# Window attention, max-MoE and gated MoE in one kernel: 256x256 weight tiles, a 16-bit sign word, low parts on VectorE, and another order

## The chip, the core and the metric

The kernel runs on one core of one Trainium2 chip. The core has a matrix engine (TensorE, PE in the profile; its weight loads are shown apart as PEld), a vector engine (VectorE, DVE), a scalar engine (ScalarE, ACT), GpSimd (POOL) and SyncE (SP), which issues nearly all DMAs here. They run side by side and wait for each other by semaphores. The metric is the device time of one execution in microseconds (us).

## What is computed

Three stages follow each other. All inputs are float64 and reach the kernel as pairs of 32-bit words; the output is float32.

```python
# attention, batch 4, 8 heads, 512 local + 32 global rows, head size 64
s_g = scale * q_g @ concat(k_g, k_l).T;  out_g = softmax(s_g) @ concat(v_g, v_l)
s_l = concat(scale * q_l @ k_g.T, where(|i-j| <= 32, scale * q_l @ k_l.T, -1e9))
out_l = softmax(s_l) @ concat(v_g, v_l)
x = concat(out_g, out_l)                     # 2176 tokens x 512
# max-MoE, d_ff 768
h = maximum(maximum(x @ w1, x @ w2), x @ w3);  x = h @ w_out
# gated MoE, d_ff 1536
out = (sigmoid(x @ w_gate) * (x @ w_val)) @ w_out2
```

## The kernel before

**Work units.** The attention is cut into 32 units: batch, half of the local rows, and pair of heads (four units make one chunk `c`; there are eight chunks). The max-MoE takes a chunk at a time, as soon as its four units are done. So the first two stages run interleaved, and the gated MoE follows them.

**A unit.** For chunks 0 and 1, TensorE transposes rows of q and k (`tq`, `tk`, L532), VectorE and ScalarE copy them out (`qw` L553, `kw` L557), TensorE makes the scores (`sp`, L619), VectorE adds the mask and takes the minimum of the negated scores (`sm`, `st`, L625: four main instructions, "reductions" below, each with an accumulator read), ScalarE takes the exponentials (L661, four) and scales their sum (L665), VectorE takes the reciprocal (L667) and multiplies (L675). TensorE transposes the result (`tp`, L683, two halves of four matmuls), ScalarE copies one half out (`pw`, L686) and VectorE the other (`pw`, L688). TensorE multiplies by the values (`ot`, L770), and ScalarE writes the unit's part of x (L790 for chunk 0, whose max-MoE runs on whole float32 values; L796 and L798 split it into a high and a low part for the others). The global rows have their own small products (`sg`, `tpg`, `ogw`).

**The weights of the max-MoE.** `w1`, `w2`, `w3` are 512 x 768 and `w_out` is 768 x 512, in float64. `conv_a(i)` brings one tile in by a DMA on SP (L302, L305) and makes it float32 in `to_f32`: ScalarE shifts the low word (L285) and scales the high word (L289), VectorE puts the sign of the high word into the low word (L291) and shifts the two together (L294). Chunk 0 uses that value. For the other chunks ScalarE rounds it to a high part (L312) and the helper `sub` subtracts the high part on GpSimd (L271), which leaves the low part; three matmuls (`mm3`, L321 to L323: high-high, high-low, low-high) then take the place of one. A tile of w1 to w3 holds all 512 rows (four blocks of 128) of 128 columns, 512 values in each of the 128 partitions. There are 24 tiles, 18 of w1 to w3 and 6 of w_out. In a product of layer 1 (`moe1_l1`, L882 for chunk 0) the four blocks of one tile meet the four parts of x; its maximum with the other two products is taken on VectorE (`h` L896, `hw` L893). Layer 2 (`moe1_l2`) follows, L918 for chunk 0. The gated MoE also uses `to_f32`, with 1024 values in a partition.

**The order.** Every step is an event, and a step issues a few instructions on their engines. The table `ORDER` at the top lists the numbers of all events; each engine runs its instructions in that order, and waits only where data or buffers are not ready. `SLOT` places the buffers.

Of the kernel before, what the change touches and what calls it, by code (L numbers as in the profile page):

```python
# [12 lines left out]
U32 = mybir.dt.uint32  # L13
AF = mybir.ActivationFunctionType
ALU = mybir.AluOpType
# [188 lines left out]
def kernel(  # L204
# [76 lines left out]
    def to_f32(raw, low_on_act, out=None):  # L281
# [4 lines left out]
        else:  # L286
            nc.vector.tensor_scalar(out=lo, in0=lo.bitcast(U32), scalar1=2.0 ** -29, scalar2=7.0, op0=ALU.mult, op1=ALU.min)
        yield
        nc.scalar.mul(f32(hi), f32(hi), 2.0 ** -112)  # L289
        yield  # L290
        nc.vector.scalar_tensor_tensor(out=lo, in0=hi, scalar=-2147483648, in1=lo,  # L291
                                       op0=ALU.bitwise_and, op1=ALU.bitwise_or)
        yield
        nc.vector.scalar_tensor_tensor(out=hi if out is None else out, in0=hi, scalar=3, in1=lo,  # L294
# [1182 lines left out]
```

## Time and profile before

| what | value |
|---|---|
| time, median of 3 runs | 809.6 us (809.15 to 814.51) |
| the profiled execution's own time | 812.87 us |
| its span, first to last instruction | 811.0 us |
| mean granted TensorE clock | 0.996 of full speed |
| PE busy | 788.9 us, 6854 matmuls |
| DVE busy | 599.6 us |
| ACT busy | 472.7 us |
| POOL busy | 148.8 us |

The span is the part that the profile resolves; 1.9 us of the execution lie around it. Times of rows are counted from the span's start. A busy PE need not be at its peak, since matmuls are pipelined. In rows of a timeline consecutive instructions of one kind are merged (x8 is eight of them; one float32 matmul of the program shows as two records). "Idle before" names what ended an engine's wait.

### The profile page before, as it was taken

What the parts mean: (1) busy time and instruction counts of PE and PEld (TensorE: products, weight loads), DVE (VectorE), ACT (ScalarE), POOL (GpSimd) and SP (SyncE); (2) the same over time, 40 slices, a digit from 0 to 9 for tenths busy, and PEclk for the clock granted to TensorE, in tenths of its full rate; (3) what the DMA queues carried; (4) which work ended last, traced back from release to release, by engine and by line L of the source; (5) the groups of instructions that cost most, each with busy time, mean ns of one, the idle gap of its engine ahead of it and who ended that gap; (6) DMA issues with size and microseconds to landing.
All of it is one profiled execution on the core that took longest, in us unless ns stands there. A gap on an engine that the chain in (4) does not pass through costs nothing.

```text
span 811.0 us, 18055 instructions
## 1 busy us (share of the span) xinstructions
PE 788.9 (97%) x6854; PEld 751.8 (93%) x6854; DVE 599.6 (74%) x1291; ACT 472.7 (58%) x1131; POOL 148.8 (18%) x149
## 2 busy tenths in 40 slices
PE   5999998999999999999999999999999999999998
PEld 3687798998999999899999999999999999999998
DVE  4799895876767676874876888788675858967773
ACT  6897775756446664563647656665636366444442
POOL 3241565243332413332120000000000000000000
PEclk9899999999999999999999999999999999999999
DMA  8998254545556553453425355956422469555411
GB/s 202 265 248 212 60 101 87 102 93 104 107 101 109 96 113 66 101 117 75 181 90 191 101 158 175 317 175 231 147 101 91 163 207 311 166 162 164 142 34 58
DMA packets 217590, 116.07 MB, mean 143 GB/s; under 512 B 161056, under 2 KB 204576, under 8 KB 217504
## 3 DMA queue, kind: packets, MB, share of 16 engines
q1 hardware_dynamic: 216960, 114.80, 52.2%
q8 instruction: 53, 0.87, 0.5%
q14 instruction: 33, 0.27, 0.1%
q10 hardware_dynamic: 544, 0.13, 0.1%
HBM read 74.91 MB, written 28.57 MB: 128 GB/s over the span
## 4 chain that ended last, share of the span: by engine, by line
PE 73%; SPq 8%; issue 6%; DMA 5%; DVE 3%; POOL 2%; ACT 2%; DVEq 0%; POOLq 0%; ACTq 0%
PE pa L1038 18%; PE pe L1038 9%; PE pa L1225 9%; PE ps L321 7%; PE ps L323 7%; PE ps L322 6%; PE pb L1038 4%; PE pe L1225 4%; PE pb L1225 2%; SPq L514 2%; SPq L513 2%; PE sp L619 2%; DMA vr<-in_v_g_dram 1%; PE ps L918 1%; POOL m L271 1%
## 5 line engine op out<-in xcount | busy, mean ns | idle before, releaser
L1038 PE MATMUL pa<-m,m 128*128 128x384 f32 (+1 forms) x864 | 154.1, 327 | 0.0
L321 PE MATMUL ps<-xt,m 128*128 128x288 f32 (+1 forms) x504 | 147.4, 292 | 3.5 <-DVE h L896 2.2
L323 PE MATMUL ps<-xt,m 128*128 128x288 f32 (+1 forms) x504 | 146.6, 291 | 0.0
L322 PE MATMUL ps<-xt,m 128*128 128x288 f32 (+1 forms) x504 | 145.3, 288 | 1.1 <-DVE xt L798 0.9
L1038 PEld LDWEIGHTS pa<-m,m 128*128 128x128 f32 x864 | 144.3, 188 | 0.2
L321 PEld LDWEIGHTS ps<-xt,m 128*128 128x128 f32 x504 | 94.8, 188 | 7.8 <-issue 2.7
L322 PEld LDWEIGHTS ps<-xt,m 128*128 128x128 f32 x504 | 94.7, 188 | 1.5 <-DVE xt L798 1.1
L323 PEld LDWEIGHTS ps<-xt,m 128*128 128x128 f32 x504 | 94.7, 188 | 0.0
L1044 ACT COPY sn<-pa 128x384 f32<-128x384 f32 (+1 forms) x108 | 49.0, 462 | 73.0 <-PE pa L1038 72.6
L1038 PE MATMUL pe<-m,m 128*128 128x384 f32 (+1 forms) x432 | 80.2, 327 | 0.0
L1038 PEld LDWEIGHTS pe<-m,m 128*128 128x128 f32 x432 | 72.5, 188 | 0.1
L1225 PE MATMUL pa<-m,m 128*128 128x256 f32 x576 | 71.9, 283 | 0.0
L1225 PEld LDWEIGHTS pa<-m,m 128*128 128x128 f32 x576 | 70.4, 192 | 0.1
L661 ACT ACTIVATE sm<-sm,st 128x224 f32<-128x224 f32 x128 | 60.8, 481 | 13.3 <-DVE st L625 13.0
L896 DVE TENSOR_TENSOR h<-ps,h 128x288 f32<-128x288 f32 (+1 forms) x90 | 38.9, 436 | 34.9 <-PE ps L323 23.5
L271 POOL TENSOR_TENSOR h<-h,h 128x288 fp32r<-128x288 f32 (+1 forms) x42 | 39.4, 942 | 103.1 <-ACT h L901 102.6
L707 DVE TENSOR_TENSOR pc<-sm,pc 64x512 f16<-64x512 f32 (+1 forms) x72 | 52.0, 723 | 8.1 <-ACT pc L704 6.9
L625 DVE CUSTOM_DVE_ANT_0 sm<-sp,mask 128x224 f32<-128x224 f32 x128 | 44.9, 381 | 7.9 <-PE sp L619 7.4
L321 PE MATMUL ps<-h,m 128*128 128x288 f32 (+1 forms) x168 | 49.4, 294 | 0.0
L1163 ACT CAST m<-m 128x768 fp32r<-128x768 f32 x44 | 35.8, 835 | 23.0 <-DVE m L1174 7.5
L704 ACT CAST pc<-sm 64x512 f16<-64x512 f32 (+1 forms) x72 | 39.3, 545 | 16.7 <-DVE sm L675 15.1
L323 PE MATMUL ps<-h,m 128*128 128x288 f32 (+1 forms) x168 | 48.9, 291 | 0.0
(193 smaller groups left out, 1628.7 us busy)
## 6 DMA issues: line engine op xcount, KB each, us to landing
m<-in_moe_w_dram SPq DMA_DIRECT2D x18, 512.0 KB, 5.5
gd<-sgt SPq DMA_DIRECT2D x48, 192.0 KB, 2.8
m<-gd SPq DMA_DIRECT2D x6, 1536.0 KB, 7.3
m<-in_moe_w_val_dram SPq DMA_DIRECT2D x6, 1024.0 KB, 5.3
wr<-in_moe_w_out_dram SPq DMA_DIRECT2D x6, 1024.0 KB, 6.0
m<-in_moe_w_gate_dram SPq DMA_DIRECT2D x5, 1024.0 KB, 7.6
vr<-in_v_l_dram SPq DMA_DIRECT2D x48, 96.0 KB, 2.5
x2d<-x2s SPq DMA_DIRECT2D x32, 128.0 KB, 2.0
```

The costliest lines, as they stand in the source:

```text
L271: nc.gpsimd.tensor_tensor(out=out, in0=a, in1=f32(b), op=ALU.subtract)
L321: nc.tensor.matmul(ps, lhsT=wh, rhs=xh, start=first, stop=False)
L322: nc.tensor.matmul(ps, lhsT=wh, rhs=xl, start=False, stop=False)
L323: nc.tensor.matmul(ps, lhsT=wl, rhs=xh, start=False, stop=last)
L625: nc.vector.tensor_tensor_reduce(out=sm[:, hh, j], in0=sp[hh][:, j, 0:224], in1=mask[:, half + j, :], scale=-SC, scalar=3.0e38, op0=ALU.ad ...
L661: nc.scalar.activation(sm4[:, i], sm4[:, i], AF.Exp, bias=st[:, 0, i:i + 1], scale=-1.0, accum_out=st[:, 2, i:i + 1])
L704: nc.scalar.copy(d, s_)
L707: nc.vector.tensor_tensor(out=l_, in0=s_, in1=h_, op=ALU.subtract)
L896: nc.vector.tensor_tensor(out=a, in0=ps[:, 0:n], in1=a, op=ALU.max)
L1038: nc.tensor.matmul(ps, lhsT=w[l][:, a, i], rhs=x[m][:, i], start=(k in (1, 2, 5) and i + l + m == 0), stop=(k in (2, 3, 4) and i == 1 and ...
L1044: nc.scalar.copy(t[:, 0:n], pend[u]["a"][:, 0:n])
L1225: nc.tensor.matmul(ps, lhsT=g[l][:, f], rhs=wo_op(b, f, m), start=(k in (1, 2, 5) and f + l + m == 0), stop=(k in (2, 3, 4) and f == 5 and ...
```

## The change

Four things change.

1. A tile of w1 to w3 becomes 256 rows by 256 columns, still 512 values in a partition. Its DMA reads rows of 2048 bytes where it read 1024. A product of layer 1 now reads two tiles (the two row halves of a column pair), and two products share a pair. The order of tiles in the queue is that of the event table.
2. The sign step works on 16-bit words: a one-source operation copies the top half of the high word, masked to its sign bit, into the top half of the low word. It was a two-source operation on 32-bit words. The same helper serves the gated MoE.
3. The 24 subtractions that make the low parts of the max-MoE weights are issued on VectorE where GpSimd did them. The subtractions of `h` (L271) stay on GpSimd.
4. The whole table `ORDER` is another one (a first line of each stands in the diff).

```diff
-    153, 154, 57, 87, 0, 256, 56, 62, 63, 64, 67, 68, 69, 74, 58, 70, 71, 59, 1854, 161, 162, 95, 96, 75, 76, 77, 78,
+    56, 57, 0, 62, 63, 64, 67, 223, 68, 69, 74, 75, 58, 59, 70, 76, 71, 77, 5, 161, 162, 163, 6, 7, 8, 9, 171, 78, 79,
...
@@ to_f32
-        nc.vector.scalar_tensor_tensor(out=lo, in0=hi, scalar=-2147483648, in1=lo,
-                                       op0=ALU.bitwise_and, op1=ALU.bitwise_or)
+        half = raw.bitcast(U16)
+        nc.vector.tensor_scalar(out=half[:, :, 1], in0=half[:, :, 3], scalar1=0x8000, scalar2=None, op0=ALU.bitwise_and)
...
@@ conv_a
+        fp, kh = divmod(f, 2)
...
-            nc.sync.dma_start(out=raw.rearrange("p (k f) t -> p k (f t)", k=KD),
-                              in_=src[:, f * 2 * P:(f + 1) * 2 * P].rearrange("(k p) f -> p k f", p=P))
+            nc.sync.dma_start(out=raw.rearrange("p (k f) t -> p k (f t)", k=2),
+                              in_=src[kh * 2 * P:(kh + 1) * 2 * P, fp * 4 * P:(fp + 1) * 4 * P].rearrange("(k p) f -> p k f", p=P))
...
-        sub(t[:, 1], hi, t[:, 0])
-        wa[wi, f] = t.rearrange("p l (k f) -> p l k f", k=KD) if cols else t
+        nc.vector.tensor_tensor(out=t[:, 1], in0=hi, in1=f32(t[:, 0]), op=ALU.subtract)
+        wa[wi, f] = t.rearrange("p l (k f) -> p l k f", k=2) if cols else t
...
@@ moe1_l1
+        cols = slice(P * (f % 2), P * (f % 2) + P)
+        tiles = [(wi, f - f % 2 + k // 2) for k in range(KD)]
         if c in WHOLE1:
             for k in range(KD):
-                nc.tensor.matmul(ps[:, 0:n], lhsT=ww[wi, f][:, k], rhs=xt[c, k][:, 0, 0:n], start=(k == 0), stop=(k == KD - 1))
+                nc.tensor.matmul(ps[:, 0:n], lhsT=ww[tiles[k]][:, k % 2, cols], rhs=xt[c, k][:, 0, 0:n], start=(k == 0), stop=(k == KD - 1))
```

**SP, the loads at the start.** The queue before, from the first weight tile (`m<-in_moe_w`, 128x4x256: four blocks of 256 words) to the q rows of chunk 1 (`m_289`); `m_258` and `m_259` are that chunk's k rows:

```order
L302 DMA m_175<-in_moe_w_dram 128x4x256
L385 DMA qgr<-in_q_g_dram 32x4x32 x4
L302 DMA m_234<-in_moe_w_dram 128x4x256
L302 DMA m_244<-in_moe_w_dram 128x4x256
L440 DMA m_258<-in_k_l_dram 128x8x64 x2
L442 DMA m_259<-in_k_l_dram 32x8x64
L443 DMA m_259<-in_k_g_dram 32x8x64
L432 DMA m_289<-in_q_l_dram 128x8x64 x2
```

The same stretch now (`m_256`, `m_257` k rows, `m_288` q rows of chunk 1):

```order
L387 DMA qgr<-in_q_g_dram 32x4x32 x4
L304 DMA m_212<-in_moe_w_dram 128x2x512
L304 DMA m_241<-in_moe_w_dram 128x2x512
L304 DMA m_248<-in_moe_w_dram 128x2x512
L304 DMA m_250<-in_moe_w_dram 128x2x512
L442 DMA m_256<-in_k_l_dram 128x8x64 x2
L444 DMA m_257<-in_k_l_dram 32x8x64
L445 DMA m_257<-in_k_g_dram 32x8x64
L434 DMA m_288<-in_q_l_dram 128x8x64 x2
```

Four weight tiles stand ahead of chunk 1's rows where three stood.

**PE, from a late transpose (`tp`) of chunk 0's units to the first two products of layer 1.** Before (`m_387` values, `xw` the parts of x, `m_374` and `m_175` weight tiles):

```order
L683 MATMUL tp<-ident,sm 128x128 x4
L645 MATMUL sg<-kw,qgz_82 64x256 x2
L647 MATMUL sg<-kw,qgz_82 64x32 x2
L770 MATMUL ot<-pw,m_387 64x128 x16
L619 MATMUL sp<-kw,qw 128x224 x4
L882 MATMUL ps_554<-xw,m_374 128x256 x4
L645 MATMUL sg<-kw,qgz_82 64x256 x2
L882 MATMUL ps_568<-xw,m_175 128x256 x4
```

Now (`m_389` values; `m_248`, `m_212`, `m_241`, `m_363` weight tiles):

```order
L685 MATMUL tp<-ident,sm 128x128 x8
L621 MATMUL sp<-kw,qw 128x224 x4
L647 MATMUL sg<-kw,qgz_82 64x256 x2
L772 MATMUL ot<-pw,m_389 64x128 x16
L886 MATMUL ps_544<-xw,m_248 128x256 x2
L886 MATMUL ps_544<-xw,m_212 128x256 x2
L647 MATMUL sg<-kw,qgz_82 64x256 x2
L649 MATMUL sg<-kw,qgz_82 64x32 x2
L886 MATMUL ps_575<-xw,m_241 128x256 x2
L886 MATMUL ps_575<-xw,m_363 128x256 x2
```

The scores `sp` of a unit of chunk 1 now stand ahead of the last value product of chunk 0, and each product of layer 1 takes two tiles.

**DVE, around the reductions of the fourth unit (unit 3) of chunk 0.** Before, from the reciprocal and multiplication of unit 2 on; the reductions are those of unit 3, `pw` is unit 1's, and `qw` belongs to chunk 1:

```order
L667 RECIPROCAL st<-st 128x4
L675 TENSOR_TENSOR sm<-sm,st 128x896
L625 ISA sm,st<-sp,mask 128x224
L625 ISA st 128x1
L688 COPY pw<-tp 128x512
L553 COPY qw<-tq 128x256
```

Now, from the reciprocal of unit 2 to its multiplication; the reductions are again those of unit 3:

```order
L669 RECIPROCAL st<-st 128x4
L690 COPY pw<-tp 128x512
L555 COPY qw<-tq 128x256
L627 ISA sm,st<-sp,mask 128x224
L627 ISA st 128x1
L627 ISA sm,st<-sp,mask 128x224
L627 ISA st 128x1
L627 ISA sm,st<-sp,mask 128x224
L627 ISA st 128x1
L627 ISA sm,st<-sp,mask 128x224
L627 ISA st 128x1
L677 TENSOR_TENSOR sm<-sm,st 128x896
```

The two copies that stood among the reductions now stand ahead of them, and the multiplication of unit 2 stands behind them where it stood ahead.

**DVE, up to the copy of the last transposed half of chunk 0 (`pw`, the last row of each).** Before, from the first weight step behind the copy of unit 2:

```order
L291 SCALAR_TENSOR_TENSOR m_374<-m_374 128x512
L625 ISA sm,st<-sp,mask 128x224
L625 ISA st 128x1
L625 ISA sm,st<-sp,mask 128x224
L625 ISA st 128x1
L294 SCALAR_TENSOR_TENSOR m_374<-m_374 128x512
L688 COPY pw<-tp 128x512
```

Now:

```order
L293 TENSOR_SCALAR m_248<-m_248 128x512
L627 ISA sm,st<-sp,mask 128x224
L627 ISA st 128x1
L627 ISA sm,st<-sp,mask 128x224
L627 ISA st 128x1
L627 ISA sm,st<-sp,mask 128x224
L627 ISA st 128x1
L293 TENSOR_SCALAR m_328<-m_328 128x512
L316 TENSOR_TENSOR m_346<-m_250,m_346 128x512
L690 COPY pw<-tp 128x512
```

Three reductions, two sign steps and one of the moved subtractions stand ahead of that copy, where two reductions, a sign step and a shift stood (one more reduction stands ahead of either piece).

## Rows read from the trace of the kernel before

**Rows 1.** Span and engines, from the page: busy us (share) xinstructions.

```profile
span 811.0 us, 18055 instructions
PE 788.9 (97%) x6854; PEld 751.8 (93%) x6854; DVE 599.6 (74%) x1291; ACT 472.7 (58%) x1131; POOL 148.8 (18%) x149
```

**Rows 2.** Busy us (and instructions) of PE, PEld, DVE, ACT, POOL by stretch; PEclk, DMA share, GB/s.

```profile
0.00:38.00 38.00, 27.63 (x191) 19.56 (x193) 23.63 (x71) 26.81 (x85) 10.78 (x29) 0.91 0.87 230
38.00:104.00 66.00, 63.33 (x443) 52.28 (x439) 60.45 (x144) 54.93 (x146) 25.78 (x19) 1.00 0.70 176
104.00:380.00 276.00, 270.23 (x3303) 254.20 (x3299) 195.43 (x578) 161.03 (x490) 103.84 (x95) 1.00 0.51 98
380.00:811.00 431.00, 427.68 (x2930) 425.77 (x2928) 320.14 (x500) 229.91 (x412) 8.37 (x8) 1.00 0.48 159
```

**Rows 3.** What PE waited for, whole span: total us, times, longest us.

```profile
PE tq L532 <- DMA m<-in_q_l_dram: 8.1, 4, 3.6
PE ps L321 <- DVE h L896: 2.2, 1, 2.2
...
PE ps L918 <- ACT vb L591: 1.3, 1, 1.3
...
PE tp L683 <- DVE pwg L744: 1.2, 1, 1.2
```

**Rows 4.** PE in order of time, 20 to 41 us: start us, us, instruction, idle before.

```profile
20.95 0.48 PE L532 MATMUL tq<-ident,m 128*128 128x128 f32 x1 [0.92 <-DMA m<-in_q_l_dram]
...
22.08 1.12 PE L645 MATMUL sg<-kw,qgz 128*64 128x256 f32 x4
...
23.29 1.97 PE L683 MATMUL tp<-ident,sm 128*128 128x128 f32 x8
25.19 1.86 PE L619 MATMUL sp<-kw,qw 64*128 64x224 f32 x8
...
37.63 1.03 PE L619 MATMUL sp<-kw,qw 64*128 64x224 f32 x8
38.59 2.23 PE L882 MATMUL ps<-xw,m 128*128 128x256 f32 x8
```

**Rows 5.** DVE in order of time, 27 to 36 us.

```profile
27.08 0.39 DVE L625 CUSTOM_DVE_ANT_0 sm<-sp,mask 128x224 f32<-128x224 f32 x1 [2.05 <-PE sp L619]
...
27.40 0.69 DVE L688 COPY pw<-tp 128x512 f32<-128x512 f32 x1
28.00 0.41 DVE L553 COPY qw<-tq 128x256 f32<-128x256 f32 x1
...
31.76 0.68 DVE L688 COPY pw<-tp 128x512 f32<-128x512 f32 x1
32.36 0.38 DVE L625 CUSTOM_DVE_ANT_0 sm<-sp,mask 128x224 f32<-128x224 f32 x1
...
34.98 0.68 DVE L688 COPY pw<-tp 128x512 f32<-128x512 f32 x1
```

**Rows 6.** DVE groups, 0 to 110 us: xcount | busy us, mean ns | idle before.

```profile
L291 DVE SCALAR_TENSOR_TENSOR m<-m 128x512 int32<-128x512 int32 x24 | 19.5, 819 | 1.7 <-ACT m L289 1.6
L294 DVE SCALAR_TENSOR_TENSOR m<-m 128x512 int32<-128x512 int32 x24 | 19.1, 813 | 0.3
```

**Rows 7.** Groups of DVE and POOL, whole span.

```profile
L291 DVE SCALAR_TENSOR_TENSOR m<-m 128x1024 int32<-128x1024 int32 x11 | 13.4, 1221 | 5.3 <-ACT m L289 5.3
L595 DVE CAST vb<-vr 128x512 bf16<-128x512 f32 x24 | 10.5, 440 | 16.4 <-POOL vr L593 13.1 <-DMA qr<-in_q_l_dram 3.1
...
L1015 DVE TENSOR_TENSOR m<-m,m 128x512 fp32r<-128x512 f32 x11 | 7.6, 688 | 3.4 <-ACT m L1011 3.3
...
L271 POOL TENSOR_TENSOR m<-m,m 128x512 fp32r<-128x512 f32 x24 | 34.5, 1441 | 67.4 <-ACT m L312 56.8 <-DMA qr<-in_q_l_dram 10.4
```

**Rows 8.** DVE, then POOL, in order of time, at 84 us.

```profile
84.01 1.92 DVE L291 SCALAR_TENSOR_TENSOR m<-m 128x512 int32<-128x512 int32 x1
...
84.07 1.31 POOL L271 TENSOR_TENSOR m<-m,m 128x512 fp32r<-128x512 f32 x1
```

More of the change, by code (lines that the diff above doesn't have):

```diff
@@ L13 @@
 U32 = mybir.dt.uint32
+U16 = mybir.dt.uint16
 AF = mybir.ActivationFunctionType
@@ L308, in conv_a @@
         hi = f32(raw[:, :, 1])
-        ww[wi, f] = hi.rearrange("p (k f) -> p k f", k=KD) if cols else hi
+        ww[wi, f] = hi.rearrange("p (k f) -> p k f", k=2) if cols else hi
         yield
@@ L879, in moe1_l1 @@
         ps = ps_mm.tile([P, CH], F32, tag="mm", name="ps1")
+        cols = slice(P * (f % 2), P * (f % 2) + P)
+        tiles = [(wi, f - f % 2 + k // 2) for k in range(KD)]
         if c in WHOLE1:
             for k in range(KD):
-                nc.tensor.matmul(ps[:, 0:n], lhsT=ww[wi, f][:, k], rhs=xt[c, k][:, 0, 0:n], start=(k == 0), stop=(k == KD - 1))
+                nc.tensor.matmul(ps[:, 0:n], lhsT=ww[tiles[k]][:, k % 2, cols], rhs=xt[c, k][:, 0, 0:n], start=(k == 0), stop=(k == KD - 1))
         for k in range(KD) if c not in WHOLE1 else ():
-            wt = wa[wi, f]
+            wt = wa[tiles[k]]
             x = xt[c, k]
-            mm3(ps[:, 0:n], (wt[:, 0, k], wt[:, 1, k]), (x[:, 0, 0:n], x[:, 1, 0:n]), k == 0, k == KD - 1)
+            mm3(ps[:, 0:n], (wt[:, 0, k % 2, cols], wt[:, 1, k % 2, cols]), (x[:, 0, 0:n], x[:, 1, 0:n]), k == 0, k == KD - 1)
         yield
```

336 rows, old and new, of the table ORDER are left out of this document.

## The prediction

> **What bounds the kernel now.** I read the page's engine table first [rows 1]: PE is busy 788.9 of 811.0 us, DVE 599.6. So PE sets the time, and what can be won is PE's idle time, 811.0 − 788.9 = 22.1 us, plus whatever PE does at a low clock.
>
> The second view cuts the span at three places where PE's work changes kind [rows 2]: about 38 us, where the first layer-1 product of chunk 0 starts, about 104 us, where the first three-matmul products start, and 380 us, behind which PE is 99% busy to the end. PE idles 38.0 − 27.6 = 10.4 us in the first stretch, 66.0 − 63.3 = 2.7 in the second, 276.0 − 270.2 = 5.8 in the third and 431.0 − 427.7 = 3.3 in the last. The granted clock is 0.91 in the first stretch alone and 1.00 behind it. DVE is busy 60.5 of 66.0 us in the second stretch, with 5.5 us of air; in the third it has 276.0 − 195.4 = 80.6. PE issues the same matmuls before and after the change, so the time moves only by this idle time and by the clock.
>
> The third view names the waits [rows 3]: 8.1 us for q rows (`tq`), then single ones of 2.2 (`h`), 1.3 and 1.2 us. The timelines show the start in order: the last `tq` wait ends at 20.95, and from there PE and DVE hand work to each other until the first product at 38.59 [rows 4, 5].
>
> **The start, to the first product.** Up to the transposes of chunk 1's q rows the DMAs set the pace: DMA share 0.87, 230 GB/s [rows 2]. SP now sends four weight tiles ahead of those rows where it sent three. A tile is 128 × 1024 words of 4 bytes, 512 KB, and takes 524 KB / 230 GB/s = 2.3 us, so the transposes that started at 20.95 start near 23.2.
>
> From there I rebuild the chain from the rows. To the global scores 1.1 us (20.95 to 22.08), to the end of `tp` which precedes the scores 3.1 (22.08 to 25.19) [rows 4]. Before, unit 3's scores stood behind this and DVE waited 2.05 us for them [rows 5]. Now scores of units 2 and 3 stand ahead of the late q rows, so the wait goes; but the two copies `pw` and `qw`, 0.69 + 0.41, now stand ahead of the first reduction. `tp` needs only its first half for `pw`: 23.2 + 1.1 + 1.9 = 26.2, and with the copies the reductions start near 27.2, against 27.08. That is +0.1: the extra tile eats what the earlier scores win.
>
> Then, four steps:
> - First reduction to unit 2's `pw`: 31.76 − 27.08 = 4.7 us. The two copies (1.1) are out of it; the multiplication that now stands behind the reductions fits under ScalarE's exponentials. I take −0.7, with ends −1.1 and 0.
> - Unit 2's `pw` to unit 3's: 34.98 − 31.76 = 3.2 us [rows 5]. That was the copy 0.6, three reductions at 0.3 (27.08 to 27.40), a sign step 0.6, and the rest, 1.1, a shift that met GpSimd. Now it is the copy, four reductions, two sign steps of 0.4 to 0.6 (below) and a subtraction of 0.6: 3.2 to 3.6. I take +0.1, ends −0.5 and +0.5.
> - Unit 3's `pw` to the product: 38.59 − 34.98 = 3.6 us, of which scores of chunk 1 take 0.96 (37.63 to 38.59) [rows 4]. They now stand ahead of the wait for `pw`, so −1.0.
> - The first product took 2.23 us and `sp` pieces of the same stretch between 1.03 and 1.86 [rows 4]. It now needs two tiles. I take −0.3, with both there and the clock up; were the second late, all of PE's queue (the global scores, the next products and chunk 1's transposes) would wait behind it.
>
> Sum 0.1 − 0.7 + 0.1 − 1.0 − 0.3 = −1.8. The upper bound is +1.3: the extra tile's 2.3 come through whole and the other steps give half of their 1.9. The lower is −4: the half clock of this stretch goes too (`sp` x8 takes 1.86 us at 25.19 and 1.03 at 37.63, so about 0.8 is lost in each such piece, and `tp` at 23.29 with 1.97 is another) [rows 4].
>
> **38 to 104 us: weight work on DVE.** All 24 tiles are made here. Before, DVE paid 24 × (0.819 + 0.813) = 39.2 us busy, 38.6 by the grouped busy times [rows 6]. Alone on the memory these operations take about 0.69 (the same two-source kind at 128x512) [rows 7], and the row at 84.01 shows why the mean is higher: a sign step took 1.92 us while GpSimd's subtraction of 1.31 us ran [rows 8]. After: shifts 24 × 0.69 = 16.6. Sign words: no row has a one-source 16-bit operation; the nearest are the one-source cast of the same shape, 0.44, and the two-source 0.69 [rows 7]: 24 × 0.44 to 0.69 = 10.6 to 16.6. Subtractions: 24 on DVE, of which 14 stand ahead of the first three-matmul products, at 0.69: 9.7. Total 36.9 to 42.9, so DVE's queue changes by −1.7 to +4.3, against 5.5 us of air. I take the cast's 0.44, since it is the row with one source in SBUF. GpSimd's 34.5 us of subtractions [rows 7] go, and with them their hold on DVE. They waited 56.8 us for ScalarE's rounding there [rows 7]; on DVE such a wait would hold the reductions and copies queued behind it, and then PE. In the order other work stands between a tile's shift and its subtraction, so I take no stall; the air covers up to 5.5 us of them.
>
> A rule here: the Trainium skill, "VectorE: DVE Perf Modes", section "What auto-detection actually checks", has a single-source operation run two elements a cycle when source and destination are in SBUF with suitable outer dimensions, whatever the word. By it the sign word costs about what the cast costs, and the total is 36.9; if the 16-bit stride spoils it, 42.9. No run here shows which yet.
>
> What a PE wait is worth here: the stretch has 2.7 us of idle, of which 1.3 and 1.2 are single waits for late helpers behind the delayed DVE [rows 3]. I take −1.5, ends −2.7 (all) and +1.5 (DVE's 4.3 late, less part of its air).
>
> A rule that speaks against the change: the Trainium skill, "SBUF — State Buffer", section "Who interferes with whom", says that DVE with two SBUF inputs, or in its two-port modes, and a reading GpSimd instruction block each other wholly. The rows at 84 us agree (1.92 against 0.69) [rows 8]. It credits taking subtractions off GpSimd, but also says the new sign word and subtraction are of the blocking kinds and will meet what GpSimd keeps; that is rival B's cover, priced there from rows.
>
> **104 us on.** The remaining 10 subtractions (10 × 0.69 = 6.9 us) fall in 80.6 us of DVE air and cost nothing; without that air they would cost 6.9. The 5.8 us of PE idle hold the 2.2 us wait for `h` [rows 2, 3]. The order is new here too; I take −1.0, ends −5.8 and +4. Behind 380 us cheaper sign steps (1.22 us at 128x1024 [rows 7]) change nothing, since PE is 99% busy; the 3.3 us there are the tail and stay. The longer DMA rows move the same bytes; no row shows a tile of that shape alone, and I cost them at nothing; were they faster or slower by a tenth, the four tiles ahead of chunk 1's rows would move 4 × 2.3 × 0.1 = 0.9 us either way.
>
> **Sum.** −1.8 − 1.5 − 1.0 = −4.3 on the profiled 812.87 us (1.9 beyond its span). That execution is 3.3 above the median of 809.6; taken off the median, 805.3, which I round to **805.0 us**.
>
> **The rivals.**
>
> *A: no gain.* The extra tile's 2.3 us come through to the first product (+2.3 − 1.9 = +0.4) and the waits behind it only change their names: 810.0. For it: DMA at 0.87 sets the start, and nothing shortens it. Against it: the scores really move ahead of the wait.
>
> *B: VectorE becomes the bound, slower.* In 38 to 104 us the operations keep the contended price, because `h`'s subtractions and the value splits stay on GpSimd: 24 × 0.82 + 24 × 0.81 + 14 × 0.82 = 50.6 us against 38.6, +12.0, less 5.5 of air = 6.5, and the tile's 2.3: +8.8, 818.4. It decides from a mean sign step or shift of about 0.8 us on. Against it: 34.5 us of GpSimd work is what made them long.
>
> *C: a large gain.* The start keeps the full clock (−2.6 more, three such pieces of 0.8 and a bit) and 5.7 of the 8.5 us of PE idle between 38 and 380 go instead of 2.5: −4.3 − 2.6 − 3.2 = −10.1, 799.5. For it: every wait named there stands behind delayed DVE work. Against it: waits tend to be replaced by the next.
>
> *The change does not do what it says*: if the sign word takes as long as the old one, 0.69 alone, the total is 42.9 and the air covers it; that ends in A.
>
> **How the numbers follow.** Forecast (its own range 802 to 808) 0.52, A 0.20, C 0.19, B 0.09. About 1%, 8.1 us, is what a measurement of this kernel can tell from no change, given 809.15 to 814.51. Faster than that, below 801.5: C and a little of the forecast's low edge, 0.24. Slower, above 817.7: B, 0.09. Within: 0.67. The ends of the terms add up to −4 − 2.7 − 5.8 = −12.5 and +1.3 + 1.5 + 4 = +6.8, so 797 to 816; that range leaves out B and a few hundredths below.
>
> **What would show it.** Right: the first product of layer 1 starts near 36 to 37 us; the 16-bit sign step's group has a mean near 0.44; shifts fall from 0.81 to about 0.7; no DVE instruction of 128x512 takes 1.9; the waits of 1.2 and 1.3 us are gone; GpSimd is busy some 114 us. Wrong: a first product at 40 us or later (A), DVE idle near nothing between 38 and 104 us with PE waiting for weight tiles (B), or PE idle below 12 us in all (C).

## The result, and the profile after

The changed kernel takes 816.68 us (median of 10 runs, 810.82 to 818.74), the kernel before 810.34 (median of 10, 807.97 to 814.51). The ratio is 1.006 with a 95% interval of 1.0031 to 1.009: slower by 0.6%; the medians lie 6.3 us apart. The prediction said 805.0.

The 10 times fall apart by the mean granted clock that the profiler lists with each: three of the four from 810.82 to 813.20 us have 0.998 (812.15 has 0.995), the six from 816.17 on have 0.994 or less. The profiled execution, 817.59 us, is one of the six.

Span and engines of the changed kernel, from the page (before: [rows 1]):

```profile
span 815.8 us, 18026 instructions
PE 795.4 (98%) x6854; PEld 755.8 (93%) x6854; DVE 609.5 (75%) x1315; ACT 471.6 (58%) x1131; POOL 113.8 (14%) x125
```

PE's idle time fell, from 22.1 to 815.8 − 795.4 = 20.4 us, and the kernel became slower: the same 6854 matmuls keep PE busy 6.5 us longer. So the first thing to look at is the clock. The same stretches as in [rows 2] (columns as there):

```profile
0.00:38.00 38.00, 29.24 (x201) 20.84 (x203) 25.80 (x82) 29.26 (x96) 6.88 (x27) 1.00 0.96 246
38.00:104.00 66.00, 62.46 (x431) 51.74 (x431) 61.55 (x148) 52.11 (x134) 6.46 (x4) 0.97 0.64 168
104.00:380.00 276.00, 272.01 (x3212) 254.49 (x3210) 198.96 (x585) 160.26 (x487) 92.74 (x87) 0.99 0.52 98
380.00:816.00 436.00, 431.69 (x3030) 428.73 (x3024) 323.19 (x501) 230.01 (x414) 7.68 (x8) 1.00 0.48 158
```

Before, the clock was low in the first stretch (0.91), where PE had little to do. Now it is full there and low in the two middle ones, where PE is the bound. What PE waited for, whole span (before: [rows 3]):

```profile
PE tq L534 <- DMA m<-in_q_l_dram: 4.5, 1, 4.5
PE tp L685 <- DVE sm L677: 2.5, 2, 1.4
PE tpg L740 <- ACT pwg L744: 2.5, 1, 2.5
PE sp L621 <- DVE st L627: 2.1, 2, 1.4
...
PE ps L922 <- DVE m L295: 1.0, 1, 1.0
```

Of the waits of before, 8.1 us for q rows became 4.5, and those of 2.2 (`h`) and 1.2 us (`pwg`) are gone. The one of 1.3 us at the first layer-2 products (`ps` L918, 90.7 us) is still there, as the last row (`ps` L922, 91.1 us, 1.0). The second row was 0.7 before and lies in the start. The new ones are the third row and the longer wait of the fourth.

SP issues chunk 1's q rows a little earlier now (first row: the changed kernel; second: the kernel before):

```profile
15.68 1.12 SPq L434 DMA_DIRECT2D m<-in_q_l_dram  x2
16.25 1.08 SPq L432 DMA_DIRECT2D m<-in_q_l_dram  x2
```

The clock falls behind the two new waits; busy time in the stretches around them (columns as above):

```profile
58.00:62.00 4.00, 1.48 (x10) 1.12 (x9) 4.00 (x11) 4.00 (x10) 0.00 (x0) 1.00 0.42 93
62.00:66.00 4.00, 4.00 (x24) 3.06 (x22) 3.37 (x6) 0.82 (x3) 0.00 (x0) 0.58 0.02 4
294.00:298.00 4.00, 2.56 (x24) 1.75 (x24) 3.09 (x14) 2.07 (x9) 0.00 (x0) 1.00 0.64 144
298.00:305.00 7.00, 7.00 (x88) 6.03 (x87) 2.79 (x6) 2.06 (x10) 0.00 (x0) 0.51 0.48 91
```

In each pair PE first stands still for a while at full clock, and then works without a pause at 0.58 and 0.51, that is almost wholly at the lower level (1.2 of 2.4 GHz). The trace's clock records give 62.6 to 66.0 and 298.1 to 305.0 us, 10.3 us together. The profile of before has 6.8 us of half clock, 20.5 to 27.3. At half clock half of such a time is lost, so 5.2 us now and 3.4 before. The clock thus makes 1.7 of the 6.5 us by which PE's busy time grew; these rows do not resolve the rest, since a busy PE need not be at its peak.

**The place near 59 us.** PE in order of time, from the first product of layer 1 on (start us, us, instruction, idle before):

```profile
35.95 2.00 PE L886 MATMUL ps<-xw,m 128*128 128x256 f32 x8
...
58.43 0.60 PE L740 MATMUL tpg<-ident,eg 128*128 128x128 f32 x4
61.56 0.33 PE L740 MATMUL tpg<-ident,eg 128*128 128x128 f32 x1 [2.52 <-ACT pwg L744]
61.72 2.74 PE L886 MATMUL ps<-xw,m 128*128 128x256 f32 x8
```

And ScalarE at that time:

```profile
58.74 0.63 ACT L314 CAST m<-m 128x512 fp32r<-128x512 f32 x1
59.28 1.22 ACT L286 ACTIVATE m<-m 128x512 uint32<-128x512 uint32 x2
60.40 0.65 ACT L290 ACTIVATE m<-m 128x512 f32<-128x512 f32 x1
60.94 0.56 ACT L744 COPY pwg<-tpg 128x512 f32<-128x512 f32 x1
```

The five transposes `tpg` of the global probabilities write two of the three PSUM buffers of their pool, the fifth into the second. The first four are done at 59.03. The fifth starts at 61.56, right behind the end of ScalarE's copy `pwg` of the first four (60.94 and 0.56); in the run **fix_pwg** below it again starts right behind that copy. Which buffer is still held until then is not shown. The copy starts at 60.94, since the new order puts a rounding (`L314`), two weight shifts (`L286`) and a scale (`L290`) ahead of it, work that PE is not waiting for. Behind the wait a product of eight records takes 2.74 us, at half clock.

**The place near 294 us.** ScalarE, GpSimd, VectorE and PE there, from their timelines:

```profile
289.77 0.62 ACT L593 CAST vb<-vr 128x512 bf16<-128x512 f32 x1 [2.15 <-DMA vr<-in_v_g_dram]
...
290.47 1.17 POOL L595 TENSOR_TENSOR vr<-vr,vb 128x512 f32<-128x512 f32 x1 [4.89 <-ACT vb L593]
...
292.18 1.55 POOL L599 TENSOR_TENSOR vb<-vr,vb 128x512 bf16<-128x512 f32 x1 [0.54 <-DVE vb L597]
...
291.67 0.43 DVE L597 CAST vb<-vr 128x512 bf16<-128x512 f32 x1 [2.35 <-POOL vr L595]
292.01 2.26 DVE L709 TENSOR_TENSOR pc<-sm,pc 64x512 f16<-64x512 f32 x2
...
295.54 0.39 DVE L627 CUSTOM_DVE_ANT_0 sm<-sp,mask 128x224 f32<-128x224 f32 x1 [0.49 <-DVE pc L709]
...
296.30 1.64 PE L621 MATMUL sp<-kt,qt 64*128 64x224 f32 x8 [1.44 <-DVE st L627]
```

It is read from the bottom up: PE's scores wait for the reductions, these stand behind VectorE's subtractions `pc`, one of which takes 1.57 us of the 2.26 beside GpSimd's `L599`; those stand behind the cast of v, which waits for GpSimd, which waits for ScalarE, which waits 2.15 us for the DMA of v.

**VectorE's weight work**, groups from 0 to 110 us (xcount | busy us, mean ns | idle before; [rows 6]), the last from the whole span:

```profile
L293 DVE TENSOR_SCALAR m<-m 128x512 uint16<-128x512 uint16 x24 | 18.6, 792 | 0.6 <-ACT m L290 0.6
L295 DVE SCALAR_TENSOR_TENSOR m<-m 128x512 int32<-128x512 int32 x24 | 16.4, 691 | 0.4
L316 DVE TENSOR_TENSOR m<-m,m 128x512 fp32r<-128x512 f32 x17 | 11.6, 689 | 0.8 <-ACT m L314 0.7
...
L293 DVE TENSOR_SCALAR m<-m 128x1024 uint16<-128x1024 uint16 x11 | 14.8, 1347 | 2.8 <-ACT m L290 2.8
```

The 16-bit sign step has a mean of 0.79 us; the old one had 0.82 beside GpSimd [rows 6]. At 1024 values it takes 1.35 where the old one took 1.22 [rows 7]. The shift fell from 0.81 to 0.69.

**Where the lead went.** For each trace I give every matmul the usual distance to the next of its shape (the lower quartile of these distances), add these up, and read when the same amount of work has begun. The table is the difference to the profiled execution of the kernel before (minus is ahead), at times of that execution. It holds the runs of the next section as well.

```
time in before, us      42     62     86    104    286    302    409    773
changed kernel        -2.7   -3.7   -0.8    0.0   -0.6   +4.3   +3.3   +4.8
  a second profile    -2.6   -3.6   -0.7   +0.2   +0.2   +2.1   -0.1   +1.5
order_only            -2.7   -4.0   -0.8   +0.4   +0.2   +5.8   +4.9   +6.0
new_tiles_order       -3.5   -4.4   -0.8   +0.7   +1.9   +6.5   +5.5   +6.8
new_subs_gpsimd       -3.6   -4.5   -2.6   -0.1   -0.2   +1.0   -0.2   +0.3
ops_only              -0.5   +0.1  +13.1  +13.5  +13.1  +13.3  +12.1  +12.1
fix_pwg               -2.4   -3.4   -3.7   -2.9   -3.3   +3.0   +1.3   +3.0
filler                -2.3   -3.4   -1.9   -1.1   -2.8   +4.6   +2.3   +3.9
fix_both              -3.0   -4.0   -4.3   -3.5   -4.7   +0.2   -1.9   -0.4
fix2                  -3.3   -4.3   -4.7   -3.8   -6.9   -6.1   -6.5   -5.1
fix2_sign32           -2.5   -3.3   -3.7   -3.2   -4.9   -4.1   -4.7   -3.6
before_again          -0.3   -0.3   -0.3   -0.3   -1.4   -1.5   -2.6   -2.6
```

With the median or the mean as the usual distance the columns 42, 104 and from 286 on stay within 0.1. Those at 62 and 86 move, by up to 4.0 and 1.7 us: there the orders have different kinds of work behind them, and 62 lies next to a wait.

The changed kernel is 3.7 us ahead at 62 us by this measure, loses 2.9 at the first place (2.5 of wait and half of 3.4 us of half clock, less 1.2 that the kernel before loses on its own wait for `pwg` [rows 3]) and 4.9 at the second (1.4 and half of 6.9). The firmer columns give 2.7 ahead at 42 us and level at 104. The second place is not in every execution: its second profile (814.17 us) has the first half-clock stretch, 62.6 to 66.0, and none near 300.

A third loss stands in the last two columns. From 409 to 773 us, in the gated MoE, the changed kernel loses 1.5 us, and the others of the table with the new order 1.1 to 1.7 (**new_subs_gpsimd** 0.5), while **ops_only** and **before_again**, in the old order, lose nothing. In the profile of the changed kernel it falls at two short waits of PE, near 535 and 692 us, which the kernel before does not have:

```profile
535.98 1.34 PE L1042 MATMUL pe<-m,m 128*128 128x384 f32 x6 [0.53 <-DVE sgt L1061]
692.84 0.85 PE L1042 MATMUL pe<-m,m 128*128 128x320 f32 x4 [0.27 <-ACT m L1211]
```

No run mended these.

### The profile page after: what moved, and what is told of

The parts are those of the page before. It is cut to its first block, busy times and chain, and to the rows that moved or that the text cites. A ratio compares the mean times of both kernels' runs of the same rounds, so it can differ in the third digit from the quotient of the medians.

```text
span 815.8 us, 18026 instructions
## 1 busy us (share of the span) xinstructions
PE 795.4 (98%) x6854; PEld 755.8 (93%) x6854; DVE 609.5 (75%) x1315; ACT 471.6 (58%) x1131; POOL 113.8 (14%) x125
## 4 chain that ended last, share of the span: by engine, by line
PE 73%; DVE 7%; SPq 7%; DMA 6%; ACT 3%; issue 3%; POOL 1%; DVEq 0%; ACTq 0%; POOLq 0%
PE pa L1042 16%; PE pa L1229 8%; PE pe L1042 8%; PE ps L323 7%; PE ps L325 7%; PE ps L324 6%; PE pe L1229 4%; PE pb L1042 4%; PE sp L621 2%; PE pb L1229 2%; DVE pc L709 2%; SPq L515 2%; SPq L516 2%; PE ps L886 1%; PE ps L922 1%
## 5 line engine op out<-in xcount | busy, mean ns | idle before, releaser
L1042 PE MATMUL pa<-m,m 128*128 128x384 f32 (+1 forms) x864 | 156.0, 326 | 0.0
L1042 PEld LDWEIGHTS pa<-m,m 128*128 128x128 f32 x864 | 144.5, 188 | 0.4 <-DVE sgt L1067 0.2
L1042 PE MATMUL pe<-m,m 128*128 128x384 f32 (+1 forms) x432 | 81.9, 327 | 0.8 <-DVE sgt L1061 0.5
L709 DVE TENSOR_TENSOR pc<-sm,pc 64x512 f16<-64x512 f32 (+1 forms) x72 | 49.4, 687 | 6.9 <-ACT pc L706 5.9
L706 ACT CAST pc<-sm 64x512 f16<-64x512 f32 (+1 forms) x72 | 39.3, 546 | 20.4 <-DVE sm L677 18.9
L272 POOL TENSOR_TENSOR h<-h,h 128x288 fp32r<-128x288 f32 (+1 forms) x42 | 36.0, 862 | 97.8 <-ACT h L905 87.1
```

The costliest lines, as they stand in the source:

```text
L272: nc.gpsimd.tensor_tensor(out=out, in0=a, in1=f32(b), op=ALU.subtract)
L706: nc.scalar.copy(d, s_)
L709: nc.vector.tensor_tensor(out=l_, in0=s_, in1=h_, op=ALU.subtract)
L1042: nc.tensor.matmul(ps, lhsT=w[l][:, a, i], rhs=x[m][:, i], start=(k in (1, 2, 5) and i + l + m == 0), stop=(k in (2, 3, 4) and i == 1 and ...
```

## Experiments

Two theories stood first. **O**: the new order puts work that nobody waits for ahead of work that PE waits for. **P**: the order is good, and the changed operations (sign word, subtractions) make VectorE late.

**order_only**: the kernel before with the new table, nothing else; in short:

```diff
-ORDER = [  # the table of the kernel before
+ORDER = [  # the table of the changed kernel
```

> The kernel before with the new order table alone: 128-column tiles, the 32-bit sign step and GpSimd's subtractions stay. Theory O (the new order places things late for PE: ScalarE's copy pwg behind weight conversions near 59 us, VectorE's cast of v ahead of work that PE waits for near 294 us, and PE runs some us at half clock behind each): 814 to 819 us, the first layer-1 product still near 36 us, a PE wait of over 1.5 us between 55 and 65 us. Theory P (the order is good, and the two changed operations make VectorE late): 803 to 808 us, no such wait.

816.91 us, ratio 1.0078 (1.0047 to 1.011). The waits of 2.8 us for `pwg` and 2.5 us for the reductions are there, with half clock at 62.5 to 65.9 and 298.0 to 304.8. The new order alone, with the old operations and tiles, makes a loss as large as the whole change; the two intervals overlap. O holds, and P falls for the new order.

**ops_only**: the old order and tiles, with both new operations.

```diff
-        nc.vector.scalar_tensor_tensor(out=lo, in0=hi, scalar=-2147483648, in1=lo, ...)
+        nc.vector.tensor_scalar(out=half[:, :, 1], in0=half[:, :, 3], scalar1=0x8000, ...)
...
-        sub(t[:, 1], hi, t[:, 0])
+        nc.vector.tensor_tensor(out=t[:, 1], in0=hi, in1=f32(t[:, 0]), op=ALU.subtract)
```

> The kernel before with the 16-bit sign word and the 24 subtractions on VectorE, in the old order and with the old tiles. Theory O: VectorE's queue up to 104 us stays near its old length, so 807 to 811 us, no more than 0.3% from the kernel before. Theory P: 813 to 818 us, with PE waits for VectorE in 38 to 104 us that the kernel before does not have. Under both the 16-bit sign step keeps its mean of about 0.79 us at 128x512 and the shift falls to about 0.69.

826.01 us, ratio 1.0195 (1.017 to 1.022): far above either expectation. The table shows one loss of 13 us between 62 and 86 us. What SP waited for from 60 to 95 us:

```profile
SPq L306 <- DVE m L315: 16.0, 3, 9.8
```

And PE in the same stretch:

```profile
PE ogw L814 <- DMA vrw<-in_v_l_dram: 6.6, 1, 6.6
PE tp L684 <- DVE pwg L745: 2.4, 1, 2.4
```

SP's queue stands 16.0 us at three loads of `w_out` tiles, whose buffers VectorE's subtractions free. In the old order these subtractions stand late on VectorE; on GpSimd they had a queue of their own. Behind the loads on SP stand q, k and v rows, and PE waits for those. So the order of before belongs to GpSimd's subtractions. In the changed kernel no wait of SP in this stretch names a subtraction: there the new order repairs what the moved operations would break.

**new_subs_gpsimd** and **new_sign32**: the changed kernel with one operation put back.

> The changed kernel with the 24 subtractions back on GpSimd (all else as changed). Theory O: 814 to 820 us, the PE wait near 59 us stays at 2 us or more, since ScalarE's copy stands behind the same conversions. Theory P: 808 to 812 us, the wait near 59 us gone. In both the shift and the sign step grow again beside GpSimd, by some 0.1 us each in the mean.

820.92 us, ratio 1.0112 (1.0077 to 1.0147). The median is 0.9 us above O's range. The interval overlaps that of the changed kernel, so what moving the subtractions is worth in the new order is not shown. The wait for `pwg` stays at 2.4 us, but in this profile the clock does not fall behind it: it has no half clock between 18 us and the end, and at 813.0 us it is the shortest of the six executions (the others 816.5 to 822.65). PE behind the wait, the eight records at 1.90, and the stretch from 62 us:

```profile
60.63 0.33 PE L740 MATMUL tpg<-ident,eg 128*128 128x128 f32 x1 [2.40 <-ACT pwg L744]
60.79 1.90 PE L886 MATMUL ps<-xw,m 128*128 128x256 f32 x8
```

```profile
62.00:66.00 4.00, 4.00 (x31) 3.29 (x30) 3.14 (x7) 1.07 (x3) 0.00 (x0) 1.00 0.20 52
```

VectorE's groups from 0 to 110 us:

```profile
L293 DVE TENSOR_SCALAR m<-m 128x512 uint16<-128x512 uint16 x24 | 22.3, 945 | 0.6 <-ACT m L290 0.6
L295 DVE SCALAR_TENSOR_TENSOR m<-m 128x512 int32<-128x512 int32 x24 | 20.7, 869 | 0.5
```

Beside GpSimd's subtractions both grow, by 0.15 and 0.18 us in the mean. That part of the change does what the prediction said.

> The changed kernel with the old two-source 32-bit sign step. The 16-bit step takes 0.79 us at 128x512 and 1.35 at 128x1024, the old one without GpSimd beside it 0.69 and 1.22 (rows of the two traces). Theory O: the wait near 59 us stays, 814 to 819 us. Theory P, with the sign word as its main part: 809 to 813 us. By the size alone, VectorE's busy time falls by about 24 x 0.1 + 18 x 0.13 = 4.7 us.

814.41 us, ratio 1.0052 (1.003 to 1.0075), with the wait of 2.5 us for `pwg` in place. The interval overlaps that of the changed kernel: the sign word makes no difference that these runs show.

**new_tiles_order**: both operations put back, so tiles and order alone.

> The changed kernel with the old sign step and the subtractions back on GpSimd, so the 256x256 tiles and the new order alone. Against the run with the new order alone (816.9 us) it tells the tile's shape. If the shape costs or brings nothing: 815 to 819 us, the lead at 62 us within 0.7 us of 4.0, a PE wait near 59 us of 2.4 to 2.8. If the 2048-byte rows are faster to load: the first layer-1 product is 0.5 us or more earlier than in that run.

819.25 us, ratio 1.0094 (1.0061 to 1.0127), against 1.0078 (1.0047 to 1.011) for the order alone. The intervals overlap, and at 62 us the lead is 4.4 against 4.0: no effect of the tile's shape is shown.

Then the two places themselves were mended in the changed kernel. Theory **W**: the loss sits there. Theory **S**: it comes back elsewhere. Event 270 is ScalarE's `pwg` copy, 1911 a weight shift, 1026 VectorE's cast of unit 24's v rows, 1044 the last reduction of unit 25.

**fix_pwg**

```diff
-    ... 1901, 1902, 1911, 1846, 269, 1934, 1939, 1940, 1941, 270, 1942, ...
+    ... 1901, 1902, 1846, 269, 270, 1911, 1934, 1939, 1940, 1941, 1942, ...
```

> The changed kernel with one edit of its order: ScalarE's copy pwg of the global probabilities stands right behind their transposes, ahead of the weight shift and scale that it stood behind (two events moved). Theory W (the new order's loss sits at two waits of PE, near 59 and near 294 us, with PE at half clock behind each): the wait of 2.5 us near 59 us falls below 1.5, the half-clock stretch at 62 to 66 us goes, 811 to 814 us in the median. Theory S (the lead is lost in many small places, and a mended wait comes back as the next one): 815 to 818 us, as the changed kernel.

814.91 us, ratio 1.0044 (1.0023 to 1.0064). PE there:

```profile
58.78 0.60 PE L740 MATMUL tpg<-ident,eg 128*128 128x128 f32 x4
60.28 0.33 PE L740 MATMUL tpg<-ident,eg 128*128 128x128 f32 x1 [0.91 <-ACT pwg L744]
60.45 1.90 PE L886 MATMUL ps<-xw,m 128*128 128x256 f32 x8
```

The wait is 0.91, the same eight records behind it take 1.90 instead of 2.74, and the lead passes this place whole (−3.4 to −3.7, and −2.9 at 104 us). The median is 1 us above W's span. The second place is still there in this profile, with a wait of 3.1 us for the reductions and half clock at 295.2 to 302.0. Taken by the medians alone the edit is not clear of noise: its interval overlaps that of the changed kernel.

**fix_v**

```diff
-    ... 1025, 1026, 1018, ... 1043, 1624, 1625, ...
+    ... 1025, 1018, ... 1043, ... 1044, 1026, ...
```

> The changed kernel with one other edit of its order: VectorE's cast of unit 24's v rows stands behind the reductions of unit 25 where it stood ahead of them (one event moved). Theory W: the PE wait of 1.4 us for the reductions near 294 us goes, and with it the half-clock stretch at 298 to 305 us; the runs at 816 to 819 us no longer occur, median 811 to 813. Theory S: 815 to 818 us.

815.52 us, ratio 1.0056 (1.0037 to 1.0075): a miss. The wait is 1.1 us. The profiled execution has no half clock near 300, but four of six runs still take 815.2 to 816.7.

**fix_both** and **fix_both_sign32**

> Both edits of the order together in the changed kernel. Theory W: 806 to 809 us, 0.2 to 0.5% faster than the kernel before, since the lead of 3.7 us that the changed kernel has at 62 us is then kept in part; no half-clock stretch between 40 us and the end. Theory S: 812 to 816 us.

> Both edits of the order and the old 32-bit sign step (0.69 us at 128x512 where the 16-bit one takes 0.79, 1.22 at 128x1024 where it takes 1.35). If the sign word matters beyond VectorE's idle time: 1 to 2 us below the kernel with both edits. If VectorE's idle time covers it: within 1 us of it.

810.30 us, ratio 0.9997 (0.9977 to 1.0018), and 810.62, ratio 0.9992 (0.9975 to 1.001). The loss of 0.6% is gone, the gain that W expected is not there, and the old sign step again makes no difference that shows. The profile of fix_both still has half clock at 293.3 to 300.1. That of fix_both_sign32 has none there, but at 158.0 to 161.5, behind a wait of 2.0 us for `h`: what theory S said of the next wait. What ScalarE, then PE waited for near there in fix_both:

```profile
ACT vb L593 <- DMA vr<-in_v_g_dram: 3.9, 1, 3.9
```

```profile
PE sp L621 <- DVE st L627: 1.5, 1, 1.5
```

The edit took away the wrong link, as far as this profile tells. ScalarE's cast of v waits for the DMA, and its casts for `pc` are queued behind it; VectorE's cast was only next in line.

**fix2** and **fix2_sign32**: `pwg` as before, and all three first steps of unit 24's v rows (ScalarE 1024, GpSimd 1025, VectorE 1026) behind the reductions.

```diff
-    ... 997, 1024, 1620, ... 1025, 1026, 1018, ...
+    ... 997, 1620, ... 1018, ... 1044, 1024, 1025, 1026, ...
```

> The changed kernel with the copy pwg moved as before, and near 290 us all three first steps of unit 24's v rows (ScalarE's cast, GpSimd's subtraction, VectorE's cast) behind the reductions of unit 25. In the run with both edits ScalarE's cast still stood ahead of the casts pc and waited 3.9 us for the v rows' DMA, so VectorE's pc and the reductions behind it stayed late. Theory W: with that cast out of the way the PE wait for the reductions near 290 us is under 0.5 us, no half-clock stretch between 40 us and the end in the profile, 805 to 808 us, 0.3 to 0.6% faster than the kernel before. Theory S: 809 to 812 us, with a new wait of over 1 us that drops the clock elsewhere between 100 and 400 us.

> The same with the old 32-bit sign step. Theory W: 805 to 808 us, within 1 us of the one with the 16-bit word, since VectorE has idle time where PE does not wait for it. If the 16-bit word's 4.7 us of VectorE time matter: 1 to 2 us less.

810.37 us, ratio 1.0 (0.9983 to 1.0017), and 809.92, ratio 0.9992 (0.9972 to 1.0011). In the profile of fix2 the middle stretches are at full clock:

```profile
38.00:104.00 66.00, 64.08 (x453) 54.03 (x454) 63.26 (x155) 54.18 (x143) 6.53 (x4) 1.00 0.67 172
104.00:380.00 276.00, 273.62 (x3320) 257.68 (x3319) 196.55 (x586) 160.07 (x487) 93.71 (x88) 1.00 0.51 100
```

Near 290 us PE no longer waits for the reductions, as W said; a wait of 0.8 us for `xt` (`sg` L647, 291.7 us) stands there, and one of 0.8 for the reductions at 316.6. The profile of fix2_sign32 has no half clock at all before the end. Yet both medians are that of the kernel before, not 805 to 808. They lie in S's span, but neither profile has the new fall of the clock that S spoke of. And fix_both, whose profile keeps the second place, has the same median: what that place costs in a usual execution is not shown by these pairs.

**before_again**, **before_again2** and **after_again**, a second and third profile of the kernel before and a second of the changed one, went after that.

> The kernel before, unchanged, for a second profile. If its first profiled execution lost about 2.5 us at one place: this one is 2 us or more ahead of it from that place on and 809 to 811 us in all. If the time varies in many small places: it is ahead by steps under 0.7 us each.

> The same, for a third profile: the place named by the second should show again, or the steps be small again. The wait for q rows and the half-clock stretch near 21 to 27 us are expected in it too.

> The changed kernel, unchanged, for a second profile. If the execution takes 810 to 813.5 us: a half-clock stretch near 62 us and none near 300 us. If it takes 816 to 819 us: both. The wait of 2.5 us near 59 us is there in either.

The span of before_again is 808.4 us where the first profile has 811.0. Up to 130 us the two agree within 0.3; then the second is 2.4 ahead at one place near 139 us, where the first waits 2.2 us for `h` [rows 3]. In the third profile (810.1) a wait of 1.8 for `h` and half clock at 141.1 to 144.5 stand there; the first profile, with the longer wait, has full clock behind it. In after_again half clock stands at 62.6 to 66.0 us and nowhere near 300, and it takes 814.17 us, between the two groups of times that the expectation names. So leads read against the first profile are too large by up to 2.6 us at the end. Against the second, fix2's profile ends 2.5 ahead, and that execution (807.62) is the shortest of its 12 (the longest 813.34). What costs its other executions some 2.7 us in the median stays open.

**filler**: does the clock fall because PE stands still, or for another reason that comes with this place? Seven matmuls that nothing reads, ahead of the fifth transpose.

```diff
+                for _ in range(7 if t == 5 and i == 4 else 0):
+                    nc.tensor.matmul(last[0][:, 256:384], lhsT=ident, rhs=ident, start=True, stop=True)
```

> The changed kernel with seven matmuls more, whose result nothing reads, on PE ahead of the fifth transpose of the global probabilities near 59 us, where PE waits 2.5 us for ScalarE. The wait's end stays where it is, near 61.5 us, since ScalarE sets it. If the clock falls because PE stood still, the half-clock stretch at 62 to 66 us goes and some 1.7 us of the lead stay (half of 3.4 us): the lead over the kernel before at 85 us is near 2.3 us where the changed kernel has 0.8. If the clock falls for another reason, the stretch stays and the lead at 85 us is 0.8 us or less.

PE there, then the stretch behind it:

```profile
60.44 1.83 PE L743 MATMUL ps<-ident 128*128 128x128 f32 x14 [1.04 <-DVE hw L902]
62.11 0.27 PE L744 MATMUL tpg<-ident,eg 128*128 128x128 f32 x1
62.22 1.90 PE L891 MATMUL ps<-xw,m 128*128 128x256 f32 x8
```

```profile
62.00:66.00 4.00, 4.00 (x32) 3.32 (x31) 3.66 (x7) 1.60 (x6) 0.00 (x0) 1.00 0.11 23
```

With a wait of 1.0 us and useless work where 2.5 us of wait were, the fifth transpose starts no earlier (62.11), and the clock stays full: the eight records take 1.90 again. The lead at 86 us is 1.9, near the 2.3 expected for a clock that falls because PE stood still. 811.49 us, ratio 1.002 (0.9992 to 1.0047). With work added to PE the median is some 5 us below that of the changed kernel, though the two intervals overlap a little; by the half clock alone 1.7 were to be expected. The rest is not explained by its one profile, which still has half clock at 295.0 to 305.3 behind a wait of 2.8 us for the reductions.

One profile of one run is little, since new_subs_gpsimd kept the clock without any filler. All profiles of the new order together say more. At the first place seven have a wait of 2.4 to 2.8 us, and six of these show half clock behind it; six have at most 1.04 us (filler is one), and none does. At the second place half clock stands behind waits of 1.20, 1.44, 1.45, 2.50, 2.83 and 3.10 us, and not behind 0.55, 1.03, 1.11, 1.28 and 1.35. So at these two places a standstill of PE goes before each fall, but its length alone does not decide.

## Why the prediction was wrong

- **The start, −1.8: right in sign, too small, and in part by another way.** The first product starts at 35.95 us, 2.6 earlier. The 2.3 us of the extra tile did not come: SP sends chunk 1's q rows at 15.68 us (16.25 before), and behind its first transpose of all (4.48 us), where it waits 4.5 us, PE does not wait for q rows again. The low clock of this stretch is gone too (1.00 where 0.91 stood); the prediction had that as the lower end, −4. order_only shows 2.7 at 42 us with the old operations and tiles, so this gain is the order's.
- **VectorE's weight work: one of three prices wrong.** Shifts 0.69 as taken; subtractions 0.69 where 0.69 was taken; sign word 0.79 where 0.44 was taken from the cast's row, above even the upper end. The queue up to 104 us comes to about 18.6 + 16.4 + 14 × 0.689 = 44.6 us instead of 36.9 to 42.9. No run shows that this cost anything (new_sign32): VectorE is busy 61.6 of 66 us there, and the one wait of PE in the stretch that names the weight work, 1.0 us, stands where the kernel before waits 1.3. The Trainium skill, "VectorE: DVE Perf Modes", section "What auto-detection actually checks", would give the sign word two elements a cycle; this strided 16-bit form took longer than the two-source 32-bit one, and the measurement decides.
- **38 to 104 us, −1.5 with ends −2.7 and +1.5: this step failed, at +2.6** (2.6 ahead at the first product, level at 104 us). Of the two stalls named there the one of 1.2 us went and the one of 1.3 became 1.0. What came next was not looked for on ScalarE: the step asked only whether VectorE's queue holds a late instruction ("I take no stall"), and priced a wait at its length. The new order put `pwg` behind four weight conversions on ScalarE, and PE's clock halved behind the wait. With fix_pwg the wait is 0.9 us and the half clock is gone; with filler the half clock is gone while the fifth transpose starts as late as before.
- **104 us on, −1.0 with ends −5.8 and +4: failed too, at +4.8** in the profiled execution (level at 104 us, 4.8 behind at 773) and +1.3 in the second profile. 4.9 are lost at the second place in the first of these, and some 1.5 in the gated MoE in both, where the term had nothing. The new order was taken as neutral to good without reading where the v rows' steps stand on ScalarE. And the target of this term, the 2.2 us wait for `h`, is not in every execution: of the three profiles of the kernel before two have it (2.2 and 1.8), before_again does not. The changed kernel's two profiles have no such wait at that place.
- **The sum** took "idle time of PE" as all that can be won or lost, with the clock as a gain at the start alone. The idle time did fall, by 1.7 us, while the span grew by 4.8: −2.6 + 2.6 + 4.8. A loss by half clock where PE is the bound had no term; it took 1.7 us at the first place and 3.4 at the second in the profiled execution.
- **The rivals.** None was it. B had the right sign, and its 818.4 lies 1.7 us from the time measured, but that is luck: its prices were to be contended ones, and the shift fell to 0.69, while the sign step takes its 0.79 without GpSimd's subtractions (0.945 with them); between 38 and 104 us no lack of VectorE's air shows as a new wait either. Several signs of being right came true (shifts near 0.7, GpSimd at 114 us, the first product near 36 us) beside a wrong time, since none of them looked at ScalarE. The chance of 0.67 for "within 1%" covers the result; the range, 797 to 816, ends 0.7 us short of it.
- **A rule that held**: the Trainium skill, "SBUF — State Buffer", section "Who interferes with whom", has VectorE instructions with two SBUF inputs contend with a GpSimd instruction that reads SBUF. The trace agrees: the shift is at 0.69 without GpSimd's subtractions and 0.87 with them, and `pc` took 1.57 us beside `L599`.

## What to carry to other kernels

When an order is changed, read each engine's new queue for instructions that wait for a DMA or make what is not needed yet, and that stand ahead of one PE waits for; ScalarE's queue did it here, at both places. Price a PE wait in a PE-bound stretch with the slower matmuls that can stand behind it: here 1.7 us behind a wait of 2.5, and 3.4 behind one of 1.4, though not in every execution. Take operations and order apart: the operations alone cost 1.95% in the old order, the order alone 0.8%, and two moves of a few events brought the pair back to the kernel before. Both places being mended, the gain of the start still does not show in the median, and why is open but for the 1.4 us in the gated MoE: a mended wait need not give its time back. And profile the kernel before twice: two of its profiles differ by 2.4 us at one place.

## What the runs showed of the hardware that was not expected

- The granted clock fell to its lower level behind a standstill of PE of about 2.5 us, for 3.4 us (62.6 to 66.0), and behind another for 6.9 us (298.1 to 305.0), in the middle of a kernel that keeps PE 98% busy. With useless matmuls in the first gap it did not fall, in one profile.
- Whether it falls can differ between executions of one program: the changed kernel's first profile has the stretch near 300 us, its second has not, at nearly the same wait (1.4 and 1.3 us). The longer wait is not always the one: the kernel before kept full clock behind 2.2 us in one profile and lost it behind 1.8 at the same place in another, and new_subs_gpsimd kept it behind 2.4.
- A one-source operation on 16-bit words, read and written with a stride of four words, took 0.79 us for 512 values a partition, and 1.35 for 1024; the two-source operation on 32-bit words took 1.22 for 1024.
